# Attention start-up and gate order in a fused block-sparse attention and Fourier-mixing kernel

## The chip, the cores and the metric

The kernel runs on one core of a Trainium2 chip. Its time is device microseconds (us), taken as the median of a few executions; a smaller number is better. One more execution was recorded by the hardware profiler, and every duration in this document that belongs to the kernel before comes from that one. The engines are called PE (TensorE, matrix products), PEld (its weight loads), DVE (VectorE), ACT (ScalarE), POOL (GpSimd) and SP (SyncE, which here only issues DMAs). "Gate", "cast" and "sum" below are operations of the algorithm, not of the hardware.

## The reference: what is computed

Two stages. The first is causal attention in which each query sees only some blocks of 64 keys: its own block and the three earlier blocks that score best. There are 4 batches of 8 heads, 768 positions and a head size of 64.

```
k_rep       = mean of k over each block of 64 keys            # 12 per head
gate_scores = q . k_rep, causal: later blocks get -1e9
top_idx     = the 3 best blocks of each query (own block is always seen too)
scores      = where(seen and causal, q . k / 8, -1e9)
attn_out    = softmax(scores) @ v
```

The second stage takes the attention output of a batch as a 768 x 512 matrix x and mixes it: u = x + real part of its two-dimensional Fourier transform, un = layer norm of u, and out = u + relu(un @ w_ch1) @ w_ch2, with w_ch1 of 512 x 2048 and w_ch2 of 2048 x 512.

## The kernel before

**Pairs and slots.** Heads are handled two at a time: 16 pairs, four in each batch, numbered kk = 0 to 15. The main loop (line 729) has one slot for each pair, and a slot has six positions p = 0 to 5. At every position `stage_S` (L376) computes one sixth of the pair's scores on PE (three positions for head e = 0, then three for e = 1) and ACT takes the exponential of 896 columns (L391). The score tiles have two PSUM buffers, so the scores of a position can be computed only when the exponential two positions back is done.

**The stages around it.** For each pair:
- `stage_A` (L264) transposes k (who = 1) or q (who = 0) on PE, in two halves g = 0, 1 of six blocks each (L279). From the k half in PSUM, DVE sums each block of 64 keys (L292, tile kr), and copies the sums to a block-diagonal tile (L297); the same PSUM half is then cast to fp16 into kI, the operand of the scores, by ACT (L311) and for one quarter of the early pairs by DVE (L309). The sum was written down first, and the two engines take turns on one half. From the q half, DVE copies qT (L285; from pair 8 on ACT and DVE, L287 and L288); POOL then casts it into qg, the other operand of the scores (L240).
- `stage_B` (L316) is the gate product: q times the block sums on PE (L323, ten small fp32 matmuls; L331 from pair 8 on). DVE adds the causal table cz24 (L325), finds the eight best of 12 blocks (L340, ten instructions), compares (L342) and multiplies by the table oth24 (L346), which gives gmp.
- `stage_C` (L350) transposes gmp on PE (L354), and DVE copies the result into 12 more rows of qg (L357), once for each head. With the indicator rows of kI, the score product then adds a large negative number to every block that is not seen. So the scores of a pair wait for its stage C, that for its stage B, and that for its stages A of k and q.
- `stage_AV` (L399) multiplies the exponentials with v for one head and divides by the row sums (L417, L418).
- `stage_W` (L360) runs matmuls of a zero tile whose result nobody reads ("warm" in the profile).

**The second stage as filler.** When the fourth pair of a batch is done, its Fourier stages S1 and S2, norm N, transposes T, and products M1 and M2 are queued, and `filler` (L637) places them between the attention stages: by counts of costs in a planner's clock, `feed.now`, which every stage advances by a given cost and each position by at least PACE. A Fourier or transpose unit is placed once a given gap of that clock has gone by since the unit before it. All this is settled when the program is built.

**Who sets the order.** The order on PE and POOL is the order in which the code is written. The order on DVE, ACT and SP is chosen at build time by a scheduler, which can be steered: `high_priority` prefers the instructions of a block, and `issue_after(x)` puts the instructions of a block that are on x's engine behind x. Each engine then works strictly down its list. All PSUM tiles but the scores share four buffers (tag "ps", L152).

**The order before the loop (L660 to L707).** The DMAs of pair 0's k and q go out on SP and ACT, then pair 1's on SP, then the tables cz24 and oth24 on SP, id16, ltri and ut01 on POOL. PE's own list is W(11), A(0) of k and q, W(7), B(0), A(1) of k and q, W(5), C(0), B(1), W(3), and then slot 0. In a slot, USUAL (L727) says after which position the other stages come: A1 (k of pair kk+2) at 0, AV1 (second head of the pair before) at 1, A0 (q of pair kk+2) at 2, C of pair kk+1 at 3, AV0 at 4, B of pair kk+2 at 5. In slot 6 (NORM) it differs, and slot 0 holds another W(4).

Of the kernel before, what the change touches and what calls it, by code (L numbers as in the profile page):

```python
# [118 lines left out]
def kernel(  # L119
# [28 lines left out]
    C = _consts_np()  # L148
    dr = {n: nc.inline_tensor(C[n], name=f"c_{n}") for n in C}
# [25 lines left out]
    id16 = const([128, 128], F16, "id16")  # L175
    ltri = const([128, 128], F16, "ltri")
    ut01 = const([128, 128], F16, "ut01")
# [16 lines left out]
    EARLY = 7  # L194


    LATE = 6

# [47 lines left out]
    def load_fft():  # L246
        nc.sync.dma_start(cs_sb, dr["CS"].ap().rearrange("(st p) r k -> p st r k", p=128))
        nc.sync.dma_start(ss_sb, dr["SS"].ap().rearrange("(st p) r k -> p st r k", p=128))
        for t, n in ((cd_sb, "CD"), (sdn_sb, "SDN"), (sdp_sb, "SDP")):
            nc.sync.dma_start(t, dr[n].ap())  # L250
# [13 lines left out]
    def stage_A(kk, who, g):  # L264
# [18 lines left out]
        if who == 0:  # L283
            if kk < SPLIT:
                (nc.scalar.copy if kk == LATE else nc.vector.tensor_copy)(out=d["qt"][:, cols], in_=flat)  # L285
            else:
                nc.scalar.activation(out=d["qh"][:, cols], in_=flat, func=AF.Copy, scale=QS)  # L287
                STT(out=d["ql"][:, cols], in0=flat, scalar=QS, in1=d["qh"][:, cols], op0=MULT, op1=SUB)  # L288
            if g == 1 and kk != LATE:
                cast_q(kk)  # L290
        else:
            nc.vector.tensor_reduce(out=d["kr12"][:, 6 * g:6 * g + 6],  # L292
                                    in_=ps.rearrange("p a (x c) -> p a x c", x=2),
                                    axis=mybir.AxisListType.X, op=ADD)
            if g == 1 and kk < SPLIT:
                for e in range(2):
                    nc.vector.tensor_copy(out=d["kr24"][64 * e:64 * e + 64, NB * e:NB * (e + 1)],  # L297
                                          in_=d["kr12"][64 * e:64 * e + 64, :])
            elif g == 1:
                d["krx"] = krx_t[kk % 2]  # L300
                for e in range(2):
                    r, c = slice(64 * e, 64 * e + 64), slice(NB * e, NB * (e + 1))
                    hi, lo = d["krx"][r, 0, c], d["krx"][r, 1, c]
                    nc.vector.tensor_scalar(out=hi, in0=d["kr12"][r, :], scalar1=QS, scalar2=None, op0=MULT)
                    STT(out=lo, in0=d["kr12"][r, :], scalar=QS, in1=hi, op0=MULT, op1=SUB)
            for e in range(2):
                dst, src_ = d["kI"][e][0:64, cols], flat[64 * e:64 * e + 64]
                if kk < EARLY and g == 1 and e == 1:
                    nc.vector.tensor_copy(out=dst, in_=src_)  # L309
                else:  # L310
                    nc.scalar.copy(out=dst, in_=src_)  # L311
# [4 lines left out]
    def stage_B(kk):  # L316
# [28 lines left out]
        if kk < SPLIT:  # L345
            nc.vector.tensor_tensor(out=gm, in0=gm, in1=oth24[:, 1:NST, :, :], op=MULT)  # L346
        else:
            STT(out=gm, in0=gm, scalar=QS, in1=oth24[:, 1:NST, :, :], op0=MULT, op1=MULT)
# [253 lines left out]
    def queue_batch(b, start):  # L602
# [3 lines left out]
        s1_gap = 6.0 if b else 3.5  # L606
        s2_gap = 1.8 if 0 < b < B - 1 else 1.0
        t_gap = {0: 4.0, B - 1: 6.0}.get(b, 7.5)
# [3 lines left out]
        for kt in range(NST):  # L612
            last = Unit(lambda kt=kt: stage_S2(b, kt), S2_COST, last, 2.5 if kt == 0 else s2_gap)
            units.append(last)
# [44 lines left out]
    PACE = 1.4  # L659
    with tc.manual_schedule(engines={mybir.EngineType.PE, mybir.EngineType.Pool}):  # L660
# [3 lines left out]
        nc.vector.memset(eps1, 1e-6)  # L664
        nc.scalar.activation(out=dummy1, in_=eps1, func=AF.Exp, bias=eps1)
        load_qk(1)
        nc.sync.dma_start(cz24, dr["cz24"].ap().rearrange("(st p) n -> p st n", p=128))
        nc.sync.dma_start(oth24, dr["oth24"].ap().rearrange("(st p) (e n) -> p st e n", p=128, e=2))
        nc.gpsimd.dma_start(id16, dr["ident16"].ap())
        nc.gpsimd.dma_start(ltri, dr["ltri"].ap())  # L670
        for t in kr24_t:
            nc.vector.memset(t, 0.0)
        for t in krx_t:
            nc.gpsimd.memset(t, 0.0)
# [5 lines left out]
        nc.gpsimd.dma_start(ut01, dr["ut01"].ap())  # L680
# [4 lines left out]
        for sl in range(4):  # L685
            nc.gpsimd.memset(v16_t[sl][:, :, :, 64:66], 0.0)
            nc.gpsimd.memset(v16_t[sl][:, :, :, 64:65], 1.0)
        nc.gpsimd.memset(xmid, 0.0)
        nc.gpsimd.memset(fo[0][:, :, 0:1], 0.0)
        nc.gpsimd.memset(ft[2][:, :, 0:1], 0.0)  # L690

        stage_W(11)
        stage_AA(0, 1)
        stage_AA(0, 0)
# [3 lines left out]
        stage_W(7)  # L698
        stage_B(0)
        stage_AA(1, 1)  # L700
        stage_AA(1, 0)
        load_qk(3)
        stage_W(5)
        stage_C(0)
        stage_B(1)
        cast_v(1)
        stage_W(3)  # L707
# [19 lines left out]
        USUAL = dict(A1=0, AV1=1, A0=2, C=3, AV0=4, B=5)  # L727
        NORM = dict(A1=4, AV1=1, A0=5, C=3, AV0=4, B=6)
        for kk in range(NK):
            at = NORM if kk == NORM_SLOT else USUAL  # L730
            for p in range(6):
                t_in = feed.now
                main(stage_S, 0.39, kk, p // 3, p % 3)
                filler(kk, 2 * p)
                if p == 0 and kk + 2 < NK:
                    load_v(kk + 2)
                if p == at["AV1"] and kk > 0:
                    with behind_norm(kk):
                        main(stage_AV, 0.65, kk - 1, 1)
                    after_av(kk - 1)  # L740
                if p == 1 and kk - 1 == NORM_SLOT:
                    main(stage_B, 0.35, kk + 1)
                if p == at["A1"] and kk + 2 < NK:
                    main(stage_AA, 0.7, kk + 2, 1)
                if p == at["C"] and kk + 1 < NK:
                    main(stage_C, 0.3, kk + 1)
                if p == at["AV0"]:
                    main(stage_AV, 0.65, kk, 0)
                    if kk + 2 == LATE:
                        pool_after(ft[3][:, 0, 2:3])  # L750
                        cast_q(kk + 2)
                        cast_v(kk + 2)
                if p == at["A0"]:
                    if kk + 2 < NK:
                        main(stage_AA, 0.7, kk + 2, 0)
                        if kk + 2 != LATE:
                            cast_v(kk + 2)
                    if kk == 0:
                        stage_W(4)
                    if kk + 4 < NK:  # L760
                        load_qk(kk + 4)
                if p == at["B"] and kk + 2 < NK:
                    main(stage_B, 1.05 if kk + 2 < SPLIT else 0.35, kk + 2)
                filler(kk, 2 * p + 1)
                if feed.now < t_in + PACE:
                    feed.now = t_in + PACE
# [44 lines left out]
```

## Time and profile before

| what | us |
|---|---|
| median of three runs (332.92, 334.62, 334.65) | 334.62 |
| the profiled execution's own time | 332.94 |
| its span, first to last instruction | 331.2 |
| PE busy | 311.9 |
| DVE busy | 235.7 |
| ACT busy | 180.3 |
| POOL busy | 84.7 |
| start of the first scores (slot 0) | 16.66 |
| start of slots 1, 2, 3, 4 | 24.85, 32.88, 40.84, 48.73 |
| first M1 product (the long, even part begins) | 86.95 |
| last PE instruction ends | about 327 |

The 1.7 us between the profiled execution's time and its span lie outside of what the trace covers. A line of the chain of waits gives a start, a length and who held the end back in that stretch; "issue" there is time in which the engine waited for nothing that the profile shows. A line of a stretch table gives the stretch, its length, then for PE, PEld, DVE, ACT and POOL the busy time in it with the number of instructions, then the mean granted clock of TensorE (1.00 is full speed), the busy share of the DMA engines and GB/s. In a list of an engine's instructions in order of time, the first two numbers are start and length, and the bracket tells how long the engine had been idle before and what ended that. "tp" is a transposed half of q or k, "g" the gate product, "gt" the transposed gates, "sc" the scores, "ptl" the exponentials.

### The profile page before, as it was taken

To read this page: it belongs to the slowest core of one execution; us is meant where nothing else is said; L and a number is where in the kernel's file an instruction comes from. 1 tells how busy PE (TensorE), PEld (TensorE's weight loads), DVE (VectorE), ACT (ScalarE), POOL (GpSimd) and SP (SyncE) were. 2 spreads that over 40 slices of the span, in tenths; PEclk is the share of its full clock that TensorE was granted. 3 is DMA by queue.
4 is the path that set the end of the run, shared out by engine and by line. 5 is a ranking of instruction groups with operands and counts; after the bars stand their busy time and mean duration, and the time that the engine had idled before them with its cause. 6 is when DMAs were issued, how large, how long until landed. Compare 5 with 4: busy or idle time off the path is not lost.

```text
span 331.2 us, 7008 instructions
## 1 busy us (share of the span) xinstructions
PE 311.9 (94%) x2712; PEld 202.9 (61%) x2712; DVE 235.7 (71%) x750; ACT 180.3 (54%) x276; POOL 84.7 (26%) x137
## 2 busy tenths in 40 slices
PE   8799998997889989998999989999999999999995
PEld 3567776876656666555666666656666654556442
DVE  3778889689776898999765898998457588433211
ACT  3188889789965855428486754535764302244000
POOL 8545573352481120504032030502030000000000
PEclk9999999998999999999999999999999999999999
DMA  8997999990799242425324000010000011100021
GB/s 203 230 256 186 246 136 226 155 221 7 165 188 181 54 96 75 103 70 136 99 48 97 2 0 35 32 65 32 34 2 0 2 64 63 65 1 2 32 95 63
DMA packets 85312, 31.18 MB, mean 94 GB/s; under 512 B 77736, under 2 KB 81136, under 8 KB 85280
## 3 DMA queue, kind: packets, MB, share of 16 engines
q1 hardware_dynamic: 79984, 25.88, 31.4%
q0 software_dynamic: 3552, 4.40, 8.5%
q10 hardware_dynamic: 1744, 0.46, 0.6%
q8 instruction: 21, 0.34, 0.4%
q14 instruction: 11, 0.09, 0.1%
HBM read 28.63 MB, written 6.29 MB: 105 GB/s over the span
## 4 chain that ended last, share of the span: by engine, by line
PE 73%; DVE 16%; ACT 7%; issue 1%; POOL 1%; DVEq 0%; ACTq 0%
PE ch L592 22%; PE ha L578 14%; PE sc L386 8%; PE hb L578 7%; PE av L412 5%; ACT kI L311 4%; PE g L323 3%; PE za L480 2%; DVE mx L340 2%; DVE ptl L397 2%; ACT ptl L391 2%; PE tp L279 2%; PE warm L365 2%; PE gt L354 2%; PE mx L507 2%; PE mx L508 2%
## 5 line engine op out<-in xcount | busy, mean ns | idle before, releaser
L391 ACT ACTIVATE ptl<-sc 128x896 f16<-128x896 f32 x96 | 87.3, 919 | 45.9 <-PE sc L386 36.6
L592 PE MATMUL ch<-w_sb,hT 128*128 128x512 f16 x384 | 91.4, 379 | 0.5 <-DVE qT L288 0.5
L578 PEld LDWEIGHTS <-w_sb 128*128 128x128 f16 x512 | 48.8, 97 | 38.6 <-issue 4.7
L578 PE MATMUL ha<-unT,w_sb 128*128 128x512 f16 x256 | 65.7, 378 | 1.8 <-DVE hT L583 1.4
L386 PE MATMUL sc<-qg,kI 76*128 76x512 f16 (+3 forms) x256 | 54.8, 306 | 3.6 <-ACT ptl L391 3.6
L592 PEld LDWEIGHTS <-hT 128*128 128x128 f16 x384 | 36.2, 97 | 35.1 <-issue 0.6
L581 ACT ACTIVATE hT<-ha 128x512 f16<-128x512 f32 x64 | 38.1, 597 | 33.5 <-PE ha L578 33.4
L583 DVE TENSOR_SCALAR hT<-hb 128x256 f16<-128x256 f32 x64 | 26.8, 421 | 28.9 <-PE hb L578 28.7
L578 PE MATMUL hb<-unT,w_sb 128*128 128x256 f16 x256 | 38.4, 272 | 1.1 <-ACT hT L581 0.7
L429 POOL TENSOR_TENSOR fs<-x 128x384 f16<-128x384 f16 x12 | 10.9, 909 | 105.5 <-DVE x L418 91.8
L386 PEld LDWEIGHTS <-kI 76*128 76x128 f16 x256 | 24.0, 100 | 20.3 <-issue 2.8
L311 ACT CAST kI<-tp 64x384 f16<-64x384 f32 x57 | 27.1, 475 | 14.6 <-DVE kr L292 13.6
L595 DVE TENSOR_TENSOR u<-ch,u 128x512 f32<-128x512 f32 x24 | 16.5, 685 | 19.9 <-PE ch L592 19.6
L412 PE MATMUL av<-v,ptl 128*128 128x65 f16 x672 | 26.2, 195 | 0.0
L412 PEld LDWEIGHTS <-ptl 128*128 128x128 f16 x672 | 24.8, 98 | 2.0
L292 DVE TENSOR_REDUCE kr<-tp 128x6 f32<-128x384 f32 x32 | 17.2, 551 | 7.0 <-PE tp L279 7.0
L397 DVE TENSOR_TENSOR ptl<-ptl,ut 128x384 f16<-128x384 f16 x36 | 16.0, 479 | 6.1 <-ACT ptl L391 5.7
L553 ACT ACTIVATE x<-u,nmr,rstd 128x512 f16<-128x512 f32 x12 | 8.9, 806 | 17.7 <-DVE nmr L546 17.6
L418 DVE TENSOR_TENSOR x<-av,rcp 128x384 f16<-128x384 f32 x32 | 17.8, 557 | 0.9
L390 PE MATMUL sc<-ltri,id 128*128 128x128 f16 x84 | 18.4, 219 | 0.0
L240 POOL COPY qg<-qT 64x768 f16<-64x768 f16 x16 | 14.4, 902 | 12.1 <-ACT qT L287 11.6
L520 DVE BATCH_NORM_STATS2 bst<-u 128x6 f32<-128x512 f32 x24 | 16.6, 692 | 1.2 <-ACT u L516 0.7
(112 smaller groups left out, 422.9 us busy)
## 6 DMA issues: line engine op xcount, KB each, us to landing
vn<-in_v_dram SPq DMA_DIRECT2D x32, 192.0 KB, 3.3
out_dram<-u SPq DMA_DIRECT2D x24, 256.0 KB, 2.0
kn<-in_k_dram SPq DMA_DIRECT2D x30, 192.0 KB, 3.3
qn<-in_q_dram SPq DMA_DIRECT2D x30, 192.0 KB, 3.4
w_sb<-in_moe_w_ch_dram POOLq DMA_DIRECT2D x8, 256.0 KB, 7.0
w_sb<-in_moe_w_ch_dram POOLq DMA_DIRECT2D x4, 512.0 KB, 9.5
cs_sb<-c_CS SPq DMA_DIRECT2D x1, 289.5 KB, 4.9
ss_sb<-c_SS SPq DMA_DIRECT2D x1, 289.5 KB, 5.2
```

Of the source, the lines that this page charges most:

```text
L292: nc.vector.tensor_reduce(out=d["kr12"][:, 6 * g:6 * g + 6], in_=ps.rearrange("p a (x c) -> p a x c", x=2), axis=mybir.AxisListType.X, op=ADD)
L311: nc.scalar.copy(out=dst, in_=src_)
L386: nc.tensor.matmul(sp[:, co:co + (a1 - a0)], d["kI"][e][0:76, 128 * jt:128 * (jt + 1)], d["qg"][e][0:76, a0:a1], start=True, stop=not diag)
L390: nc.tensor.matmul(sp[:, co:co + 128], id16, ltri, start=False, stop=True)
L391: nc.scalar.activation(out=pt[:, SEC * s:SEC * (s + 1)], in_=sp[:, 0:SEC], func=AF.Exp, scale=0.125 if kk < SPLIT else 0.125 / QS)
L397: nc.vector.tensor_tensor(out=dg, in0=dg, in1=um, op=MULT)
L412: nc.tensor.matmul(av[:, st, 0:65], pt[:, o:o + 128], d["v16"][:, e, jt, 0:65], start=(cnt == 0), stop=(cnt == 20))
L418: nc.vector.tensor_tensor(out=x_b[:, :, 64 * h:64 * h + 64], in0=av[:, :, 0:64], in1=rcp.to_broadcast([128, NST, 64]), op=MULT)
L578: nc.tensor.matmul(hp_, w1_sb[:, dt, 128 * it:128 * (it + 1)], unT[:, dt, c0:c1], start=(dt == 0), stop=(dt == NDT - 1))
L581: nc.scalar.activation(out=hT[:, c0:c1], in_=hp_, func=AF.Relu)
L583: nc.vector.tensor_scalar(out=hT[:, c0:c1], in0=hp_, scalar1=0.0, scalar2=None, op0=mybir.AluOpType.max)
L592: nc.tensor.matmul(cps, x["hT"][it][:, 128 * st:128 * (st + 1)], w2_sb[:, it, :], start=(it == 0), stop=(it == NIT - 1))
```

## The change

1. **Tables.** cz24 and oth24 are issued on ACT's queue, right behind pair 0's k and q, where they were on SP behind pair 1's; they, and the Fourier tables, are laid out in the order in which a partition reads them. id16, ltri and ut01 become one tile and one DMA on POOL, where they were three.
2. **Memsets.** Those of krx and of v's extra columns go from POOL to DVE; those of xmid, fo and ft stay on POOL, and move into slot 0.
3. **Before the loop.** Pair 0's stage A and gates are high priority, B(0) follows its transposes at once, the second half of pair 0's k is cast behind its q, pair 1's sums go behind pair 0's gates, and only the k half of A(1) is left there. A(1) of q and B(1) go into slot 0 (Q and B in LAYOUT). W(7), W(5), W(3) and slot 0's W(4) go; W(2) and W(4) come, so that 17 warm matmuls are left of 30.
4. **k.** From pair 2 on, the first half is cast, then summed; the second half is cast and summed by `finish_k`, written down behind the next position's scores. Pairs 0 and 1 keep the sum first. Three q copies (both of pair 1's, the second of pair 0's) go from DVE to ACT, and so does the last quarter of these two pairs' k casts.
5. **Slots.** B is now that of pair kk+1 at position 1 (it was that of pair kk+2 at position 5), AV1 moves from 1 to 2, A0 from 2 to 3; slots 0, 4, 5 and 6 have lists of their own.
6. **Planner.** PACE 1.4 to 1.3, and somewhat shorter gaps for S1, S2 and T.

(`sums_k`, not shown, holds the former lines of L292 to L305: the reduction and the copies of the block sums.)

```
+    ON_ACT = (0, 1, LATE)
...
             if kk < SPLIT:
-                (nc.scalar.copy if kk == LATE else nc.vector.tensor_copy)(out=d["qt"][:, cols], in_=flat)
+                on_act = kk in ON_ACT and (kk > 0 or g == 1)
+                d["q_out"] = (nc.scalar.copy if on_act else nc.vector.tensor_copy)(out=d["qt"][:, cols], in_=flat)
...
         else:
-            nc.vector.tensor_reduce(out=d["kr12"][:, 6 * g:6 * g + 6],
...
+            if kk < 2:
+                sums_k(kk, g, ps)
+                if kk == 0 and g == 1:
+                    d["tp_k"] = ps
+                else:
+                    cast_k(kk, g, ps)
+            elif g == 0:
+                cast_k(kk, g, ps)
+                sums_k(kk, g, ps)
+            else:
+                d["tp_k"] = ps
+
+    def finish_k(kk):
+        ps = P[kk].pop("tp_k", None)
+        if ps is not None:
+            cast_k(kk, 1, ps)
+            if kk > 0:
+                sums_k(kk, 1, ps)
+
+    def cast_k(kk, g, ps):
+        d = P[kk]
+        flat = ps.rearrange("p a c -> p (a c)")
+        cols = slice(384 * g, 384 * (g + 1))
+        for e in range(2):
+            dst, src_ = d["kI"][e][0:64, cols], flat[64 * e:64 * e + 64]
+            if 2 <= kk < EARLY and g == 1 and e == 1:
+                nc.vector.tensor_copy(out=dst, in_=src_)
+            else:
+                nc.scalar.copy(out=dst, in_=src_)
...
+        nc.scalar.dma_start(cz24, dr["cz24"].ap())
+        nc.scalar.dma_start(oth24, dr["oth24"].ap().rearrange("p st (e n) -> p st e n", e=2))
         nc.scalar.activation(out=dummy1, in_=eps1, func=AF.Exp, bias=eps1)
         load_qk(1)
-        nc.sync.dma_start(cz24, dr["cz24"].ap().rearrange("(st p) n -> p st n", p=128))
-        nc.sync.dma_start(oth24, dr["oth24"].ap().rearrange("(st p) (e n) -> p st e n", p=128, e=2))
-        nc.gpsimd.dma_start(id16, dr["ident16"].ap())
-        nc.gpsimd.dma_start(ltri, dr["ltri"].ap())
+        nc.gpsimd.dma_start(mm16, dr["mm16"].ap())
...
         stage_W(11)
-        stage_AA(0, 1)
-        stage_AA(0, 0)
+        with tc.high_priority():
+            stage_AA(0, 1)
+            stage_AA(0, 0)
+        with tc.issue_after(P[0]["q_out"].ins):
+            finish_k(0)
         cast_v(0)
         load_qk(2)
         load_v(1)
-        stage_W(7)
-        stage_B(0)
-        stage_AA(1, 1)
-        stage_AA(1, 0)
+        with tc.high_priority():
+            gates = stage_B(0)
+        with tc.issue_after(gates.ins):
+            stage_AA(1, 1)
+        stage_W(2)
+        with tc.high_priority():
+            stage_C(0)
         load_qk(3)
-        stage_W(5)
-        stage_C(0)
-        stage_B(1)
-        cast_v(1)
-        stage_W(3)
+        stage_W(4)
...
-        USUAL = dict(A1=0, AV1=1, A0=2, C=3, AV0=4, B=5)
-        NORM = dict(A1=4, AV1=1, A0=5, C=3, AV0=4, B=6)
+        USUAL = ["A1", "B", "AV1", "A0 C", "AV0", ""]
+        LAYOUT = {
+            0: ["Q", "B", "A1", "A0", "C AV0", ""],
+            NP: ["A1", "AV1", "B", "A0", "C AV0", ""],
+            NORM_SLOT - 1: ["A1", "B", "AV1", "A0 C", "AV0", "B+"],
+            NORM_SLOT: ["", "AV1", "", "C", "A1 AV0", "A0"],
+        }
         for kk in range(NK):
             for p in range(6):
                 main(stage_S, 0.39, kk, p // 3, p % 3)
+                if kk + 2 < NK:
+                    finish_k(kk + 2)
                 filler(kk, 2 * p)
...
-    PACE = 1.4
+    PACE = 1.3
-        s1_gap = 6.0 if b else 3.5
-        s2_gap = 1.8 if 0 < b < B - 1 else 1.0
-        t_gap = {0: 4.0, B - 1: 6.0}.get(b, 7.5)
+        s1_gap = 6.0 if b else 3.2
+        s2_gap = 1.8 if 0 < b < B - 1 else 1.0 if b else 0.8
+        t_gap = {0: 3.4, B - 1: 6.0}.get(b, 7.0)
```

## The prediction

> **What bounds the kernel now.** I read the busy times by stage first, then the chain of waits, then each engine's own list. The stages differ. From 86.95 us on PE works without a break but for single waits (213.8 us busy of 219.4, up to 306.3). No engine but PE is near its limit there, and the change leaves that work alone. So what is won before 86.95 stays won, if nothing is lost behind it. The stretches before are these: the start, slots 0 to 4, and slots 5 and part of 6.
>
> ```profile
> 0.00:16.66 16.66, 13.41 (x75) 8.04 (x76) 9.44 (x38) 4.42 (x8) 11.65 (x37) 1.00 0.99 217
> 16.66:24.85 8.19, 7.73 (x81) 5.72 (x80) 6.22 (x23) 6.68 (x9) 3.32 (x5) 1.00 1.13 256
> 24.85:32.88 8.03, 7.34 (x99) 6.01 (x99) 6.65 (x26) 6.71 (x10) 4.16 (x5) 1.00 0.75 181
> ...
> 48.73:62.22 13.49, 12.13 (x154) 10.55 (x154) 10.46 (x34) 10.12 (x18) 7.26 (x13) 1.00 0.99 207
> 62.22:73.43 11.21, 11.19 (x130) 9.05 (x130) 9.61 (x36) 9.90 (x16) 4.25 (x5) 1.00 0.97 189
> ```
>
> A slot of 8.03 us holds 7.34 of PE, 6.65 of DVE and 6.71 of ACT: three engines nearly full, none all of the time. The start looks busy on PE too, but much of that is warm matmuls. The chain of waits through the start shows what it really is: a row of small dependent steps.
>
> ```profile
> 7.41 1.67 PE warm L365 x7
> 9.07 1.03 PE g L323 x10
> 10.10 0.38 PE tp L279 x3
> 10.48 0.02 issue
> 10.51 1.02 DVE kr L292 x2
> 11.53 0.03 issue
> 11.56 0.28 DVE gsb L325
> ...
> 12.11 0.82 DVE mx L340 x10
> ...
> 14.49 0.46 PE gt L354 x5
> 14.95 1.24 PE g L323 x10
> ```
>
> Pair 0's gate product is done at 10.10, but its first DVE step starts at 11.56, because pair 1's sums stand ahead of it on DVE; pair 1's casts and copies then cut into the steps, and C(0) comes at 14.49. The scores start at 16.66, behind B(1) and W(3). In the slots the list of ACT shows the second loss:
>
> ```profile
> 25.55 0.92 ACT L391 ACTIVATE ptl<-sc 128x896 f16<-128x896 f32 x1 [0.67 <-PE sc L390]
> 26.74 1.48 ACT L311 CAST kI<-tp 64x384 f16<-64x384 f32 x3 [0.27 <-DVE kr L292]
> 28.11 3.66 ACT L391 ACTIVATE ptl<-sc 128x896 f16<-128x896 f32 x4
> ```
>
> The k halves are transposed at 25.29 to 25.95. The casts start at 26.74, since the sum goes first and stands behind the gate steps on DVE; then three casts in a row hold ACT for 1.48, and PE waits 0.69 for the exponential at 29.17.
>
> **The start, -4.4.** Up to 6.88 (the second sum, 5.79 + 1.09) nothing changes. DVE then has one q copy (0.56) and two sum copies (0.42): 7.9. The other q copy is on ACT, behind two casts that end at 7.36: +0.48 (an ACT copy of that shape), 7.85. W(7) is gone, so B(0) runs from 7.9, 1.1 long (8.91 to 10.10 and 9.07 to 10.10 before): 9.05. Then gsb 0.28, ten maxima 0.82, compare 0.27, multiply 0.21, with four gaps of 0.03: 10.75. C(0) 0.46: 11.2. The first copy into qg takes 0.5 (1.00 for two) and ends at 11.7, and the first scores need only head 0's; W(4) takes 4 x 0.22 and ends at 12.1. Pair 1's first sum (0.55) may stand in front of that copy: 12.25. I take 12.2, so 16.66 - 12.2 = 4.4 (rounded down). With both sums and their copies in front (1.1 + 0.35) it is 13.3: -3.4; with none, -4.6.
> What covers the rest of it: the tables go out on ACT at about 3.4 (its four loads end at 3.40) and are needed at 9.05 and 10.5. cz24 took 3.5 to land, id32, of nearly its size, 2.1, the slowest load here 3.9: at the latest 0.5 + 0.5 of issue later, at 8.3. ACT's table load (1.28, now at 3.43) and its first activation (0.29) slip by those 0.9 to 5.9; ACT's first cast was at 6.38. If that cover went, only casts would be late, which have until 12. SP loses 1.77 us of issues, so v and pair 2 come earlier. POOL issues one DMA for three (1.85 us) and loses 1 us of memsets to DVE, which was idle 4.2 us before 5.79; its q casts (1.70) then end at 9.6, before the gates. The Fourier tables are needed at 55.5 and landed 5 us after 30: nothing.
>
> **Slot 0, +1.2.** The q half of A(1) (0.65) and B(1) (1.1) come in, W(4) (0.86 paced) goes: PE +0.9. ACT is tighter: six exponentials 5.5, pair 2's casts 1.46, pair 1's two q copies 0.96 and its last two k casts 0.95 make 8.87. B(1) at position 1 stands in PE's list ahead of the next scores and waits for those q copies, so some of ACT's 1.2 idle of a slot stays; I take 0.5: 9.4 against 8.19. Ends: 8.87 with no idle (+0.7), and with the q copies behind both casts and an exponential, 10.7 (+2.5).
>
> **Slots 1 to 3, -1.4.** They take 8.03, 7.96 and 7.89. With the cast first, ACT casts from about 25.7 instead of 26.74, two casts before one exponential and one behind the next, so the wait of 0.6 to 0.7 a slot goes. What is late next is PE itself, 7.34 busy, with DVE close to it. I take 7.5 a slot: 23.88 - 22.5. Ends: 7.2 a slot (-2.2), and no gain at all, because the sums now wait for casts and DVE is as full as ACT.
>
> **Slot 4, -0.6.** It has 1.36 us of PE idle, 0.77 and 0.46 of it on ACT behind three k casts at 51.14. Half of that; ends -1.2 and 0.
>
> **Later, +0.2.** Following the planner's sums through the new lists, batch 0's units fall on the same positions as before (S1 in slot 4 at position 4, T in slot 6 at 3), later ones move by one or two units: nothing. The second k half now holds one of the four shared PSUM buffers over one more position, in slots with M1 units that use two each. The nearest row is PE's one wait for a buffer held by a copy, 0.93 at 86.56. Bounds: that wait gained, -0.9, or 0.25 more in each of eight slots, +2; one in four of that wait is 0.2.
>
> **The sum.** -4.4 + 1.2 - 1.4 - 0.6 + 0.2 = -5.0, so 332.94 becomes 327.9 against this execution's own time. It lies 1.7 below the median. About that much is the price of one stretch at half clock, and this execution shows one:
>
> ```profile
> 11.46:14.88 3.42, 1.99 (x14) 1.06 (x14) 3.30 (x19) 1.06 (x3) 0.82 (x1) 1.00 1.13 256
> ...
> 76.32:79.73 3.41, 1.85 (x25) 1.33 (x23) 3.21 (x13) 3.28 (x5) 0.00 (x0) 1.00 0.00 0
> 79.73:83.14 3.41, 3.41 (x38) 3.16 (x36) 2.91 (x9) 2.78 (x6) 1.79 (x2) 0.50 0.16 38
> ```
>
> After 3.41 us with 1.85 busy, holding one idle gap of 1.7 where T waits for the norm, the clock was 0.50 for 3.41 us, in which PE was full: 1.7 lost. After 1.99 busy of 3.42 it stayed 1.00. That stall is not touched. In the new start I count B(0) 1.1, A(1) of k 0.65, W(2) 0.43 and part of C(0) in 8.05 to 11.46, some 2.6 busy: above both rows, so 13 fewer warm matmuls cost no clock. Whether such a stretch falls once more or once less in another execution I can't tell from one trace; for the step up to the median I add a third of one, 0.6: 328.5.
>
> [...]
>
> **Rivals.**
> 1. *The loop gives it back.* Slot 0 takes its upper end and slots 1 to 4 gain nothing: -4.4 + 2.5 + 0.2 = -1.7, 331.2. For it: DVE 6.65 and PE 7.34 of 8.03, so little slack is left to win; B(1) needs ACT. Against: the casts' wait is on the chain in every slot.
> 2. *All ends well:* -4.6 + 0.7 - 2.2 - 1.2 = -7.3, 325.6, if cast and exponential interlock.
> 3. *It doesn't do what it says.* DVE's and ACT's order is the scheduler's. If it puts pair 1's sums and casts ahead of pair 0's gates again, the 4.4 shrinks to the 1.5 of W(7), and slot 0's +1.2 stands: 332.6 to 334. Against: high priority and an explicit order of DVE behind the gates.
> 4. *Gates late, slower.* B to C was six positions' work (B(2) ends at 24.8, C(2) at 29.75); now two scores, AV1 and A0 lie between, 0.55 + 0.64 + 0.55 + 0.65 = 2.4, and the DVE steps of B took 2.38 in slot 1 with sums between them. The row for C waiting behind other DVE work is 1.1, once. At 1.1 in slots 1 to 9, -5.0 + 9.9: 337.8. It is slower than the median by 0.5% from (336.3 - 327.9) / 9 = 0.93 a slot. Against: in slots 7 and on four M1 units lie between as well.
>
> **How the numbers follow.** 0.5% of 334.62 is 1.67, about what a measurement of this kernel tells from no change: faster is below 332.95, slower above 336.29. Forecast 0.55, rivals 0.20, 0.07, 0.09, 0.09. Faster: 0.55 + 0.07 + 0.18 of rival 1; same: the rest of it and rival 3, 0.11; slower 0.09. The range runs from rival 2 (325.6, taken as 325.5) to the upper part of rival 1 with a half-clock stretch, 331.2 + 1.2 = 332.4.
>
> **What would show it.** First scores at 12.2 and slot 1 at 21.6; slots 1 to 3 at 7.5 each, no wait of PE for ptl over 0.3 in them; M1 from about 82. Wrong if PE's idle before gt (L354) sums to over 3 us, if slot 0 passes 10 us, or if M1 starts early and the end does not follow.

## The result and the profile after

The changed kernel takes **338.79 us** (median of four, 338.02 to 339.60) against 334.63 for the kernel before on the same chip: a ratio of **1.0135, interval 1.0092 to 1.0179**. It is slower by 1.35%, where 328.5 and a gain were forecast. The profiled execution took 339.26 (span 337.5), against 332.94 before. Of the kernels below, b_early alone was profiled in a slow execution (337.74 against its median of 333.17, half clock from 11.27 to 24.92 us), so its start, its slot 0 and its first M1 time can't be compared.

The stretches of the changed kernel, cut where each slot's first score product starts, and below them the two stretches of 3.41 us at half clock, each with the stretch ahead of it. (Columns as before: stretch, length, then PE, PEld, DVE, ACT, POOL busy, the granted clock, DMA share, GB/s.)

```profile
0.00:14.25 14.25, 10.90 (x50) 5.60 (x51) 6.85 (x40) 5.58 (x11) 7.32 (x20) 0.88 0.96 218
14.25:23.61 9.36, 7.70 (x83) 6.08 (x82) 5.47 (x22) 6.86 (x12) 3.85 (x7) 1.00 1.06 239
23.61:32.20 8.59, 7.36 (x97) 6.01 (x98) 7.04 (x28) 6.11 (x9) 4.08 (x6) 1.00 0.78 173
...
49.28:64.11 14.83, 12.31 (x154) 10.53 (x153) 11.73 (x37) 9.94 (x16) 8.73 (x17) 1.00 1.02 195
64.11:77.53 13.42, 12.46 (x140) 10.14 (x139) 9.81 (x38) 10.92 (x18) 4.20 (x5) 1.00 0.74 148
7.44:10.85 3.41, 2.47 (x21) 2.10 (x20) 1.47 (x10) 2.55 (x7) 1.52 (x2) 1.00 1.14 259
10.85:14.26 3.41, 2.98 (x12) 1.06 (x11) 3.17 (x15) 1.85 (x4) 0.94 (x2) 0.50 1.12 254
79.12:82.53 3.41, 2.11 (x25) 1.25 (x21) 3.10 (x16) 3.41 (x6) 0.00 (x0) 1.00 0.26 59
82.53:85.94 3.41, 3.41 (x27) 2.93 (x25) 2.47 (x7) 3.27 (x6) 1.78 (x2) 0.50 0.00 0
```

The half clock is not what makes this kernel slower: in another of the four executions the mean granted clock was 1.000, and it took 338.02.

A slot of 8.59 us still holds only 7.36 of PE: the work is what it was (7.34 in 8.03), and PE waits 0.5 us more. The waits of PE in slots 1 to 3, the changed kernel first (23.61 to 49.28 us), then the kernel before. A line names the waiting instruction, what it waited for, us in total, times, and the longest:

```profile
PE gt L388 <- DVE gmp L380: 3.7, 3, 1.3
```

```profile
PE sc L386 <- ACT ptl L391: 1.8, 3, 0.7
```

The old wait is gone. A larger one has come: C (gt) now waits for the last DVE step of B (gmp) once in each slot. The lists of DVE show why; here slot 1 of the changed kernel, from the k sums (kr) to gmp:

```profile
26.12 0.56 DVE L332 TENSOR_REDUCE kr<-tp 128x6 f32<-128x384 f32 x1 [1.31 <-ACT kI L328]
26.70 0.56 DVE L326 CAST kI<-tp 64x384 f16<-64x384 f32 x1
27.28 0.56 DVE L332 TENSOR_REDUCE kr<-tp 128x6 f32<-128x384 f32 x1
27.75 0.27 DVE L359 TENSOR_TENSOR gsb<-g,cz 128x120 f32<-128x120 f32 x1
...
28.29 0.82 DVE L374 MAX8 mx<-gsb 128x8 f32<-128x12 f32 x10
...
29.82 0.21 DVE L380 TENSOR_TENSOR gmp<-gmp,oth 128x120 f16<-128x120 f16 x1
```

B's products ended at 26.36, but its first DVE step starts at 27.75: DVE first sat idle 1.31 us until ACT had cast, and then did three steps on the k halves. The page's group lines say the same of the whole run, the changed kernel first, then the kernel before (after the bar: busy us, mean ns of one, then idle time just ahead, with what ended most of it):

```profile
L328 ACT CAST kI<-tp 64x384 f16<-64x384 f32 x59 | 27.8, 472 | 5.2 <-DVE kr L332 2.3
L332 DVE TENSOR_REDUCE kr<-tp 128x6 f32<-128x384 f32 x32 | 17.6, 554 | 18.2 <-ACT kI L328 13.1
```

```profile
L311 ACT CAST kI<-tp 64x384 f16<-64x384 f32 x57 | 27.1, 475 | 14.6 <-DVE kr L292 13.6
...
L292 DVE TENSOR_REDUCE kr<-tp 128x6 f32<-128x384 f32 x32 | 17.2, 551 | 7.0 <-PE tp L279 7.0
```

Thirteen us of waiting for the other engine have moved, almost whole, from ACT to DVE.

**Where the 6.3 us between the two profiled executions lie.** Scores start 2.4 earlier (14.25); slot 0 takes 1.2 more, slots 1 to 3 together 1.8 more; from slot 4 to the first M1 product it is 41.05 against 38.22, 2.8 more; from there to PE's last instruction 243.2 against 240.1, 3.1 more; the rest is the tail (-0.2). "M1 part" below means this last long stretch.

### The profile page after: what moved, and what is told of

Same layout as the page of the kernel before. It is cut to its first block, busy times and chain, and to the rows that moved or that the text cites. A ratio compares the mean times of both kernels' runs of the same rounds, so it can differ in the third digit from the quotient of the medians.

```text
span 337.5 us, 6991 instructions
## 1 busy us (share of the span) xinstructions
PE 311.3 (92%) x2699; PEld 202.2 (60%) x2699; DVE 230.2 (68%) x755; ACT 181.1 (54%) x281; POOL 81.5 (24%) x125
## 4 chain that ended last, share of the span: by engine, by line
PE 61%; DVE 25%; ACT 8%; issue 2%; POOL 1%; DMA 1%; ACTq 1%; DVEq 0%
PE ch L626 21%; PE ha L612 11%; PE sc L420 6%; PE hb L612 6%; PE av L446 4%; DVE kr L332 3%; ACT kI L328 3%; DVE mx L374 3%; ACT ptl L425 3%; PE tp L284 2%; PE za L514 2%; PE g L357 2%; DVE ft L469 2%; DVE hT L617 2%; PE unt L596 1%
## 5 line engine op out<-in xcount | busy, mean ns | idle before, releaser
L463 POOL TENSOR_TENSOR fs<-x 128x384 f16<-128x384 f16 x12 | 10.9, 907 | 116.8 <-DVE x L452 95.7
L328 ACT CAST kI<-tp 64x384 f16<-64x384 f32 x59 | 27.8, 472 | 5.2 <-DVE kr L332 2.3
L424 PE MATMUL sc<-mm 128*128 128x128 f16 x84 | 18.6, 222 | 0.0
L391 DVE COPY qg<-gt 12x640 f16<-12x640 f16 x32 | 15.5, 483 | 1.4 <-PE gt L388 0.6
L245 POOL CAST qg<-qT 64x768 f16<-64x768 f32 x16 | 13.1, 820 | 11.1 <-ACT qT L291 7.6
```

Source lines behind the costliest of these rows:

```text
L424: nc.tensor.matmul(sp[:, co:co + 128], id16, ltri, start=False, stop=True)
```

## The experiments

First the table. "Start" is the first score product, "slot" the mean of slots 1 to 3, "M1 at" the first M1 product, "M1 part" from there to PE's last instruction. The ratio is to the kernel before on the same chip, with its interval. All kernels compute the whole reference.

| kernel | us | ratio | start | slot | M1 at | M1 part |
|---|---|---|---|---|---|---|
| before | 334.63 | 1 | 16.66 | 7.96 | 86.95 | 240.1 |
| after | 338.79 | 1.0135 (1.0092-1.0179) | 14.25 | 8.56 | 90.33 | 243.2 |
| b_early | 333.17 | 0.9985 (0.9964-1.0007) | 14.36 | 8.26 | 91.14 | 240.8 |
| sum_first | 331.93 | 0.9953 (0.9928-0.9977) | 13.24 | 7.79 | 85.38 | 240.5 |
| gates_first | 337.61 | 1.0110 (1.0063-1.0157) | 12.70 | 8.40 | 87.80 | 243.3 |
| tables_pool | 338.63 | 1.0137 (1.0092-1.0182) | 13.34 | 8.56 | 89.72 | 243.2 |
| cast_first_at_once | 337.82 | 1.0152 (1.0120-1.0184) | 14.00 | 8.94 | 90.08 | 241.9 |
| sum_first_late_half | 332.29 | 0.9952 (0.9923-0.9982) | 14.05 | 7.37 | 85.95 | 241.1 |
| sum_first_b_early | 339.11 | 1.0172 (1.0136-1.0207) | 13.00 | 9.41 | 91.24 | 241.8 |
| k_part_alone | 342.46 | 1.0285 (1.0257-1.0313) | 16.84 | 7.39 | 85.24 | 251.0 |
| gates_before_sums | 337.90 | 1.0114 (1.0051-1.0176) | 13.32 | 8.69 | 88.78 | 243.1 |
| sum_first_start_late | 332.36 | 0.9969 (0.9935-1.0003) | 15.04 | 7.79 | 86.01 | 240.5 |
| sum_first_tables_pool | 332.58 | 0.9948 (0.9917-0.9980) | 13.12 | 7.79 | 85.36 | 240.4 |
| sum_first_old_planner | 330.05 | 0.9877 (0.9805-0.9949) | 13.45 | 7.79 | 85.89 | 238.5 |
| after_old_planner | 335.49 | 1.0064 (1.0039-1.0089) | 13.73 | 8.56 | 89.64 | 239.9 |
| old_slots | 340.44 | 1.0207 (1.0175-1.0240) | 13.35 | 7.48 | 83.58 | 251.1 |
| old_slots_old_planner | 340.85 | 1.0218 (1.0192-1.0244) | 13.18 | 7.48 | 84.10 | 251.0 |
| cast_first_early | 330.31 | 0.9887 (0.9818-0.9957) | 13.36 | 7.48 | 84.62 | 240.0 |
| two_orders | 329.01 | 0.9879 (0.9833-0.9926) | 13.30 | 7.48 | 85.05 | 238.5 |

### Gates late: its place, or the order of k

Theory at first: B stands too close to C (rival 4 of the prediction). Four kernels undo one thing each.

**b_early**: B back where it was, a slot earlier (AV1 and A0 stay where the change put them; the lists of slots 0, 4, 5 and 7 follow, not shown).

```
-        USUAL = ["A1", "B", "AV1", "A0 C", "AV0", ""]
+        USUAL = ["A1", "", "AV1", "A0 C", "AV0", "B+"]
```

> The changed kernel with the gate product B back at position 5, one slot earlier (slot 0 then holds B(1) and B(2)); everything else as changed. Theory 1 (the gates are late: between B and C lies too little work, so PE waits for gmp at C, 1.25 us in each of slots 1 to 3 and 1.57 in slot 4, 5.3 in all): those waits go, slots 1 to 3 fall from 8.57 to 7.5, slot 0 grows by B(2)'s 1.1, and the time is about 338.8 - 4 = 334.5 to 335.5. Theory 2 (the late k half is what is short: its cast, sum and PSUM buffer): C's wait moves to the scores or to B and the slots stay at 8.3 to 8.6, 338 to 339. Theory 3 (the loss lies in the start: ACT's list waits for DMAs, and a half-clock stretch follows): no change, 338 to 340.

**sum_first**: the sum ahead of the cast for all pairs, both halves at once (pair 0's second half is still cast later).

```
-            if kk < 2:
-                sums_k(kk, g, ps)
...
-            elif g == 0:
+            sums_k(kk, g, ps)
+            if kk == 0 and g == 1:
+                d["tp_k"] = ps
+            else:
                 cast_k(kk, g, ps)
-                sums_k(kk, g, ps)
-            else:
-                d["tp_k"] = ps
```

> The changed kernel with k summed first and cast second, both halves at once (no late half); B stays at position 1. Theory 1 (gates late by their place alone): C still waits in slots 1 to 4, at least 1 us each, since DVE still has the k sums between; 338 to 340. Theory 2 (the cast-first order puts DVE's sums behind ACT and with them the gate steps): the gate steps come about 1 us earlier, C's wait falls under 0.3 a slot, and the time falls by 3 to 5, to 334 to 336. Theory 3: no change.

**gates_first**: B's steps preferred by the scheduler.

```
+                        with tc.high_priority():
                             main(stage_B, 1.05 if n < SPLIT else 0.35, n)
```

> The changed kernel with the gate steps of every B at high priority for the scheduler, nothing else moved: DVE's list then has the gate steps with fewer k steps between them. Theory 1 in the form that DVE's order makes the gates late: C's waits shrink from 1.25 to 0.5 or less and the time falls by 2 to 4, to 335 to 337. Theory 1 in the form that the distance of B and C is too short whatever the order: C's waits stay over 1 us, 338 to 339. Theory 3: no change.

**tables_pool**: cz24 and oth24 on POOL's queue.

```
-        nc.scalar.dma_start(cz24, dr["cz24"].ap())
...
+        nc.gpsimd.dma_start(cz24, dr["cz24"].ap())
...
```

> The changed kernel with the two causal tables issued on POOL's queue behind mm16 instead of on ACT's. Theory 3 (ACT's list stands still until 5.39 us because its table DMAs wait for earlier DMAs, which moves the table load, the casts and pair 0's q copy): ACT's table load starts at 3.4 again, the gate product of pair 0 at 7.9 instead of 8.75, the scores at 13.2 or, if the half-clock stretch goes too, 12.2 instead of 14.25; the time falls by 1 to 2, to 336.8 to 337.8. Theory 1 alone: what the start wins is kept, the slots stay at 8.57. If POOL's indicator DMAs come too late instead, the first scores wait for them and nothing is won.

Either of the first two takes the loss away; sum_first beats the kernel before by 0.5%. Preferring the gates shortened the C waits of slots 1 to 3 from 3.7 to 2.3 us and gained nothing that the intervals can tell. The tables gained nothing. So the place of B and the order of k lose only together, and the next runs take the order of k apart. The slots are a part of it alone: of what sum_first gains over the changed kernel, 2.3 us lie in slots 1 to 3, 1.9 from slot 4 to the first M1 product (where the changed kernel has its second stretch of half clock) and 2.7 in the M1 part; for b_early, all of it at full clock, it is 0.9, 2.4 and 2.4.

**cast_first_at_once**: cast first, the second half no longer held back. **sum_first_late_half**: the second half still held back, but both halves summed first (the first half's two lines change places in the same way, not shown).

```
-            else:
-                d["tp_k"] = ps
+            else:
+                cast_k(kk, g, ps)
+                sums_k(kk, g, ps)
```

```
     def finish_k(kk):
...
-            cast_k(kk, 1, ps)
             if kk > 0:
                 sums_k(kk, 1, ps)
+            cast_k(kk, 1, ps)
```

> The changed kernel with both k halves cast first and summed second at once, with no half left for the next position; B at position 1. Theory 2a (the order is what costs: DVE's sum waits at the head of DVE's list for ACT's casts, and the gate steps stand behind it): DVE still idles over 8 us for the casts, C still waits about 1 us a slot, and the time stays at 1.008 to 1.014 of the kernel before. Theory 2b (the late half costs: it comes a position later and holds a PSUM buffer): the loss goes, 0.99 to 1.00. Run sum_first, which undid both, came to 0.995.

> The changed kernel with the sum first and the cast second in both halves, but the second half still left for the next position; B at position 1. Theory 2a (order): DVE idles under 2 us for casts, 0.995 to 1.00 of the kernel before. Theory 2b (late half): C still waits over 1 us a slot and the time is 1.008 to 1.014.

Holding the second half back is innocent: with the sum first and the half late the slots take 7.37, with the cast first and nothing late 8.94. It is the order of the two engines on a half. As a whole sum_first_late_half is no faster than sum_first (0.9952 and 0.9953): its profile shows half clock from 10.84 to 17.67, and its slot 0 took 10.74.

**gates_before_sums**: in slots 1 to 4 the sums and the late cast go behind B's steps in DVE's list.

```
+                        gates = stage_B(n)
+                        feed.spend(1.05 if n < SPLIT else 0.35)
+                        sums_behind(kk + 2, gates)
...
+            with tc.issue_after(gates.ins):
+                cast_k(kk, 1, ps1)
+                sums_k(kk, 0, ps0)
+                sums_k(kk, 1, ps1)
```

> The changed kernel, cast first and B at position 1 as changed, with one thing moved: in slots 1 to 4 (pairs 3 to 6) the sums of k, and the cast of its late half, stand in DVE's list behind the gate steps of that slot, not ahead of them. Theory 2a (the gate steps come late because they stand in DVE's list behind sums that wait for ACT's casts): C's wait of 1.25 in slots 1 to 3 and 1.57 in slot 4 falls under 0.4 each, slots 1 to 3 from 8.57 to 7.4 to 7.8, and the time falls by 3 to 5, to 1.000 to 1.005 of the kernel before. Rival (B and C are too near, whatever the list): C still waits over 1 us a slot and nothing is won.

The wait of C went, and the slots stayed at 8.69. From 22.85 to 49 us PE now waited for something else, with the same count:

```profile
PE tp L284 <- DVE kr L347: 2.9, 3, 1.0
```

The transposes of q now wait for the k sums, that is, for PSUM buffers that the unsummed halves hold. The stall that came from DVE's idle time was not cured by reordering DVE's list: it came out at the next thing that DVE releases.

### Both halves of the pairing

**k_part_alone**: the kernel before with only the new order of k (cast first, second half late). **sum_first_b_early**: sum_first with B a slot earlier, as in b_early.

```
+            if kk < 2:
+                sums_k(kk, g, ps)
...
+            elif g == 0:
+                cast_k(kk, g, ps)
+                sums_k(kk, g, ps)
+            else:
+                d["tp_k"] = ps
```

> The kernel before with only the new order of k (from pair 2 on cast first, second half a position later); start, tables and B's place as before. Theory 2a with 1 (order costs where the gates have no room): DVE idles 5 to 10 us for casts, but B is six positions from C, so PE waits little at C; 1.000 to 1.008 of the kernel before. If the prediction's step was right and only the place of B spoils it, PE's waits for the exponentials (2.2 us in slots 1 to 3) go and it is faster, 0.993 to 0.998.

> The changed kernel with the old order of k (sum first, at once) and the old place of B (position 5, a slot earlier); what is left of the change is the start, the tables, the memsets and the planner's numbers. If the place of B costs on its own (theory 1, distance), C's remaining waits (1.24 us in slots 0 to 4 of run sum_first) go and it is 1 us faster than that run, about 0.992 of the kernel before. If the place costs only together with the cast-first order, it is the same as that run, 0.995, or slower, since slot 0 then holds two gate products.

With all stages at their old places, cast first takes 7.39 a slot: the prediction's 7.5 comes true where the change's own slot order is absent. DVE in slot 1 of k_part_alone:

```profile
24.73 0.28 DVE L348 TENSOR_TENSOR gsb<-g,cz 128x120 f32<-128x120 f32 x1 [0.51 <-PE g L346]
25.05 0.82 DVE L363 MAX8 mx<-gsb 128x8 f32<-128x12 f32 x10
...
26.22 0.22 DVE L369 TENSOR_TENSOR gmp<-gmp,oth 128x120 f16<-128x120 f16 x1
27.04 0.56 DVE L321 TENSOR_REDUCE kr<-tp 128x6 f32<-128x384 f32 x1 [0.59 <-ACT kI L317]
```

While ACT casts, DVE does the gate steps of a B that stands ahead of A1; then it sums. In sum_first B stands behind A1, and DVE sums while PE does B. The opposite mix loses as much as the changed kernel (its 9.41 is the mean of 11.07, with a stretch of half clock in it, 8.62 and 8.55): in sum_first_b_early ACT's casts wait for sums that stand behind gate steps, and PE for the exponentials behind those casts (23 to 52 us):

```profile
PE sc L414 <- ACT ptl L419: 4.6, 3, 2.3
```

But the M1 part of k_part_alone is 10.9 us longer, and it is the slowest of all. That is taken up below.

### What the start is worth

**sum_first_start_late**: nine more warm matmuls ahead of the scores. **sum_first_tables_pool**: tables on POOL's queue.

```
-        stage_W(4)
+        stage_W(13)
```

> Run sum_first with nine more warm matmuls ahead of the first scores, so that the loop starts 9 x 0.22 = 1.9 us later (up to 3.9 if they run at half clock). If an earlier start counts in full at the end, as the prediction took it, the time is 1.9 to 3.9 longer than sum_first, 1.001 to 1.007 of the kernel before; if the loop swallows it, it stays at 0.995.

> Run sum_first with the two causal tables issued on POOL's queue, so that ACT's list doesn't wait for DMAs ahead of its table load. Theory 3 (that wait costs in the start): pair 0's gate product starts 0.9 earlier and the time falls by 0.6 to 1, to 0.992 to 0.994 of the kernel before. In run tables_pool the PE's end came 0.6 earlier, but the timed runs showed no gain; if the start's clock decides, it is the same as sum_first, 0.995.

The scores came 1.8 us later, M1 0.6 later, the end 0.6 later: slot 0 shrank from 9.60 to 8.45. Of a delay at the first score a third arrives, by these two profiles. The tables change nothing here either.

### The planner, and the M1 part

**sum_first_old_planner** and **after_old_planner**: PACE and the gaps of the kernel before.

```
-    PACE = 1.3
+    PACE = 1.4
...
-        t_gap = {0: 3.4, B - 1: 6.0}.get(b, 7.0)
+        t_gap = {0: 4.0, B - 1: 6.0}.get(b, 7.5)
```

> Run sum_first with the planner's numbers of the kernel before (PACE 1.4 and the longer gaps). The prediction took these numbers for nothing: 0.993 to 0.998 of the kernel before, the same as sum_first. If they matter, units of the filler stand elsewhere and the time moves by more than 1 us.

> The changed kernel with PACE and the gaps of before. If the planner's numbers cost the 2 us that they cost with the sum first, whatever the order of k: about 336.5, the part behind the first M1 product 241.2 instead of 243.2, slots 1 to 3 unchanged at 8.5 to 8.6. If that loss belongs to the cast-first order (buffers held until DVE is through): 338.5 to 339, that part still 243.

In both the M1 part shrinks, by 2.0 and by 3.3 us, with the slots unchanged. Of the changed kernel's whole time it is 3.3 by the medians (338.79 to 335.49), 2.4 by the two ratios. PE's waits in the M1 part, in the changed kernel and then in after_old_planner:

```profile
PE hb L612 <- DVE qT L294: 1.6, 1, 1.6
PE ch L626 <- DVE qT L294: 1.3, 1, 1.3
PE ch L626 <- DVE hT L617: 1.1, 1, 1.1
...
PE mx L541 <- DVE u L629: 0.7, 1, 0.7
PE ch L626 <- DVE u L629: 0.7, 1, 0.7
```

```profile
PE ch L626 <- DVE hT L617: 1.1, 1, 1.1
...
PE mx L541 <- DVE u L629: 0.2, 1, 0.2
```

The gaps decide between which stages an M1 or M2 unit falls; with the new ones two of them fell where DVE was still busy with a q half (qT), and PE stood 1.6 and 1.3 us at them.

**old_slots**: the changed kernel with every stage of a slot at its old position; **old_slots_old_planner**: the old gaps as well.

```
-        USUAL = ["A1", "B", "AV1", "A0 C", "AV0", ""]
+        USUAL = ["A1", "AV1", "A0", "C", "AV0", "B+"]
...
```

> The changed kernel with every stage of a slot at its position of before (A1 0, AV1 1, A0 2, C 3, AV0 4, B of pair kk+2 at 5); the start, the cast-first order and the planner's new gaps stay. If cast first needs B a slot early and nothing else: slots 1 to 3 at 7.4 to 7.5, first M1 product before 85, about 331 to 333 if the part behind it stays near 242. If k_part_alone's slots came from its older start: 8.3 a slot, as in b_early, about 333.5 or more. If cast first with B early also brings stretches of half clock behind the first M1 product, as in k_part_alone: that part above 246, and 336 or more.

> As old_slots, with PACE and the gaps of before as well. If k_part_alone's three stretches of half clock come with cast first and the old gaps: the part behind the first M1 product near 250, 339 or more. If they came from where its units happened to fall against POOL's copies: near 240, and 329 to 331.

Slots of 7.48, the earliest M1 product of all (83.58), and an M1 part of 251: as in k_part_alone, whatever the gaps. So the pairing of the early slots is right and something else is lost, three times. One of the three, in old_slots: a stretch with PE hardly busy and DVE full, and the next at half clock; then DVE's list and POOL's in it.

```profile
92.43:95.84 3.41, 1.32 (x7) 0.66 (x7) 3.41 (x11) 0.94 (x2) 2.88 (x3) 1.00 1.23 227
95.84:99.25 3.41, 3.41 (x14) 1.63 (x12) 0.92 (x3) 1.38 (x2) 1.72 (x3) 0.50 0.62 118
```

```profile
92.94 0.85 DVE L376 TENSOR_TENSOR gmp<-gsb,mx 128x120 f16<-128x120 f32 x1
...
93.98 0.90 DVE L382 SCALAR_TENSOR_TENSOR gmp<-gmp,oth 128x120 f16<-128x120 f16 x1
...
95.07 0.41 DVE L617 TENSOR_SCALAR hT<-hb 128x256 f16<-128x256 f32 x1
```

```profile
92.83 1.91 POOL L245 COPY qg<-qT 64x768 f16<-64x768 f16 x2 [0.65 <-ACT qT L293]
...
93.71 1.04 POOL L245 COPY qg<-qT 64x768 f16<-64x768 f16 x1
```

(The first POOL line holds both copies, the second line is the later one again; the earlier took 0.82.) The two gate steps take 0.27 and 0.28 elsewhere; beside POOL's copies they take 0.85 and 0.90. The copies end at 93.65 and 94.75, the steps at 93.79 and 94.88: each 0.13 to 0.14 us behind a copy. The hT of 95.07, which frees PE's buffer, stands behind them, and PE waits 1.45 us for it; 0.82 us more had gone on the hT before it, ahead of these steps. In the other two stretches it is the folds (L469, 0.55 elsewhere, 1.17 and 1.18 here) and the causal masks (L431, 0.35 elsewhere, up to 0.97 here) that are long, beside POOL's copies and, for the masks, its casts of v too. PE waited 2.27, 2.04 and 2.15 us for DVE in the three stretches of old_slots; with 1.7 of half clock behind each (3.41 us at 0.50, with PE full), that makes about the 11, by this estimate.

The times of the stretched steps follow the copies: a gate step that began during a copy ended 0.14 or 0.13 us behind it, a mask 0.2, a fold 0.4 (behind a copy or a cast of v), which is each step's own usual length less some 0.14 us and not some share more. That the copies hold the steps up is the author's reading of these times; no run moved POOL's copies alone.

**cast_first_early**: old_slots_old_planner with the cast first for pairs 2 to 7 alone. **two_orders**: the same, and from slot 6 on the changed kernel's positions.

```
-            if kk < 2:
+            if kk < 2 or kk >= SPLIT:
                 sums_k(kk, g, ps)
```

```
+        FIRST = ["A1", "AV1", "A0", "C", "AV0", "B+"]
         LAYOUT = {
-            0: ["Q", "B", "A1", "A0", "C AV0", ""],
+            0: ["Q", "B", "A1", "A0", "C AV0", "B+"],
+            1: FIRST, 2: FIRST, 3: FIRST, 4: FIRST, 5: FIRST,
```

> old_slots_old_planner with the cast first for pairs 2 to 7 alone; from pair 8 on (prepared from slot 6 on) the sum is first again. If the loss behind the first M1 product is that of the later pairs' cast-first order: slots 1 to 3 still 7.4, first M1 product near 84, the part behind it near 240 as in the kernel before, no stretch in which PE is busy under 1.4 of 3.41: 328.5 to 330. If the old positions or the earlier start of that part do it: still near 250, 339 or more.

> Cast first with the old positions in slots 0 to 5; from slot 6 on the sum first with the changed kernel's positions (B at 1); the gaps of before. If each part keeps what it had alone: slots 1 to 3 at 7.4, first M1 product at 83.6 to 84.1, then the 238.5 of the sum-first kernel with the old gaps: 328 to 329, under the 330.05 of that kernel. If the two orders don't join (the early gain is swallowed as soon as PE is the bound): 330 or more.

Both do in the main what was expected of them; cast_first_early ended just above its 328.5 to 330, and the first M1 product of two_orders came at 85.05 where 83.6 to 84.1 stood, behind a stretch of half clock from 75.58. With the sum first again from pair 8 on, the 11 us are gone (240.0), and the gate steps take 0.27 to 0.28 in the whole M1 part. Its 36 causal masks there still take 0.48 us on the mean, as in the kernel before (old_slots 0.50, the changed kernel 0.35), two of them 1.87 together from 113.27, beside POOL's copies, and no half clock follows there (granted clock 1.00 from 110 to 130 us). two_orders joins slots of 7.48 to the 238.5 of the sum-first M1 part: **329.01 us**, 1.2% under the kernel before. Its start and first two slots:

```profile
0.00:13.30 13.30, 9.80 (x50) 5.17 (x51) 6.14 (x38) 4.79 (x10) 7.33 (x20) 1.00 0.93 215
13.30:23.24 9.94, 8.61 (x93) 7.19 (x93) 6.56 (x25) 8.06 (x13) 4.20 (x8) 1.00 1.02 231
23.24:30.88 7.64, 7.38 (x99) 5.99 (x99) 7.19 (x28) 6.59 (x10) 3.89 (x5) 1.00 1.04 231
```

PE is now 7.38 busy of 7.64. Whether it is faster than sum_first_old_planner (330.05) the intervals don't tell.

## Why the prediction was wrong, step by step

The sum was 327.9 against the execution's own time, and 339.26 came: 11.4 more. The terms, measured against the profile after: start +2.05, slot 0 0.0, slots 1 to 3 +3.2, slot 4 to the first M1 product +3.4, M1 part +2.9, tail -0.2.

**The step that failed first: slots 1 to 3, -1.4.** It took the cast-first order and the new place of B as two edits and priced the first alone. It was right about that one: the wait for the exponential went, and 7.39 to 7.48 a slot came out in k_part_alone and old_slots. With B behind A1 the same order made DVE idle 1.31 us and then late. "No gain at all, because the sums now wait for casts" stood there as the step's worst end; the case was worse, 25.7 against 23.9. Rival 4 had the right wait (C for gmp, 1.2 a slot; the sum of 3.7 in slots 1 to 3 passes the 3 us set as the sign) and half of the reason. B a slot earlier does take the wait away (b_early), but 2.4 us of work between B and C are nearly enough in sum_first too, where C waits 0.7 in these three slots together; only in slot 4 does it still wait 1.43. What made the gates late in slots 1 to 3 was DVE's idle time ahead of the sums. Rival 4's price was wrong as well: it let the wait run through slots 1 to 9, but C waits only in slots 1 to 4 (5.3 in all).

**The start, -4.4.** It was -2.4 here. ACT's queue shows one slip, in the changed kernel:

```profile
2.34 1.05 ACTq L227 DMA_DIRECT2D qn<-in_q_dram  x2
5.39 0.35 ACTq L699 DMA_DIRECT2D cz<-c_cz  x1
5.78 0.44 ACTq L700 DMA_DIRECT2D oth<-c_oth  x1
6.25 1.28 ACT L701 ACT_TABLE_LOAD   x1 [6.25 <-DMA qn<-in_q_dram]
```

The prediction had cz24 issued at 3.4 and let ACT's table load slip by 0.9. The issue waited 2 us until pair 0's first load on that queue had landed (5.37; 4.68 in the kernel before), so the table load slipped to 6.25 and the first cast to 7.75. The rest is the half clock from 10.85 to 14.26, which stretched W(4) to 1.79 (four of 0.22 were counted) and C(0) to 0.72:

```profile
11.91 0.72 PE gt L388 x5
12.64 1.79 PE warm L399 x4
14.43 0.22 PE sc L420
```

In gates_first that stretch did not fall (granted clock 1.00 from 7.00 to 13.82), and the scores started at 12.70. The prediction's reason for ruling it out, some 2.6 us of PE busy in 3.41, was no bound: the stretch ahead (7.44 to 10.85) held 2.47, more than the 1.99 that had kept its clock. (The gap in the prediction's row of 1.85 was 1.56, not 1.7.) But the start matters less than its term: of 1.8 us only 0.6 reached the end (sum_first_start_late), and putting the tables on POOL's queue won nothing. "What is won before 86.95 stays won" held there only from the first M1 product on (0.6 at it, 0.6 at the end): slot 0 takes most of what the start wins.

**Slot 0, +1.2.** 9.36 for 9.4. The total was right, its working was not: it counted B(1) in and forgot that B(2) goes out. PE's work in slot 0 stayed the same (7.70 against 7.73), and ACT was busy 6.86, not 8.87, since pair 1's last k casts were over at 14.31. What made the slot long was PE idle for 1.66, for DVE in the main: 0.8 for a k sum (the line below), 0.5 for C's copies into qg, and 0.2 for ACT's q copy.

```profile
PE av L446 <- DVE kr L332: 0.8, 1, 0.8
```

**Slot 4 and on, -0.6.** The same oversight: one B less in slots 0 to 4 means one more in slot 5, 1.1 us that no term held. The rest is C waiting 1.6 us in slot 4 and the Fourier products waiting for DVE (0.8 and 0.7).

**Later, +0.2, and "later ones move by one or two units: nothing".** They were not nothing: the new gaps cost 2.4 to 3.3 of the changed kernel's time (after_old_planner), more than the 1.8 that slots 1 to 3 lost. The buffer held by the late k half, which was priced, did nothing that the time shows (sum_first_late_half).

**What stays open.** Why B alone a slot earlier takes 8.3 a slot (b_early) where all stages at their old positions take 7.4: AV1 and A0 were not moved one at a time. Why sum_first and b_early win 2.7 and 2.4 us in the M1 part though their gaps are the new ones. Why cast first from pair 8 on puts the steps ahead of hT beside POOL's copies with the old positions. And by which rule the gaps move a unit onto a busy DVE: only these two sets of numbers were run, and with old_slots they make no difference.

## What to carry to other kernels

When two engines take turns on one buffer, choose the order by what the second engine has to do meanwhile, and price it together with the order of the stages: in the early slots cast first won with the old order of the stages (7.4 to 7.5 a slot against 8.0) and lost with the new one (8.6 against 7.8). When idle time moves to another engine, reordering that engine's list can move the stall to the next thing it releases, as it did here. Numbers that only "move units by a place or two" need a run of their own, and when a stage is moved across slots, count what leaves each slot as carefully as what enters it.

## What the runs showed of the hardware

- In old_slots the gate steps and folds on DVE took two to three times as long beside POOL's copies (0.27 to 0.85, 0.28 to 0.90, 0.55 to 1.17), and PE waited 1.45 to 2.15 us for the hT behind them.
- Half clock for 3.41 us followed stretches of 3.41 us with 1.32 us of PE busy (old_slots, 92.43), 2.11 (the changed kernel, 79.12) and once with 2.47 (the changed kernel, 7.44); the longest idle gap of PE in the first was 1.45 us. Full clock followed 2.74 (gates_first, 7.00 to 10.41), but also 1.78 and 1.98 in the changed kernel (178.10 to 181.51, 58.63 to 62.04). So busy time does not sort these rows, and no threshold comes out of them; the six stretches under 1.4 in k_part_alone and old_slots (0.98 to 1.32) were all followed by half clock.
- The issue of cz24 on ACT's queue began at 5.39 us, 2.0 us behind the end of the issue ahead of it (3.39) and 0.02 us behind the landing of pair 0's first load on that queue (5.37); ACT's table load behind it began at 6.25, and at 3.43 in the kernel before.
